# Query and key rows of 14 tokens per partition, and scores, masks and values laid out with heads for batches

## The chip, the core and the metric

The program runs on one core of one Trainium2 chip. The core has five engines that this text speaks of: TensorE (PE; its weight loads are shown as PEld), VectorE (DVE), ScalarE (ACT), GpSimd (POOL) and SyncE (SP), and 16 DMA engines that move data between device memory and the on-chip memory of 128 partitions. Matmuls write to a small second memory, PSUM. The metric is the device time of one execution in microseconds, the median of several runs.

## The reference

Attention with an extra term in the softmax denominator, and then a mixture of experts with soft slots over all its tokens. The shapes: 8 batches, 12 heads, 448 tokens, 64 numbers to a head; 8 experts of 4 slots, hidden size 1024.

```
scores = q @ k^T / 8
m = max(scores, -1);  e = exp(scores - m)
attn = e / (sum(e) + exp(-m) + 1e-9);   a = attn @ v
x = a with heads side by side                     # 3584 x 768
logits = x @ phi                                  # 3584 x 32
d = softmax of logits over tokens;  slot_in = d^T @ x
slot_out[e] = relu(slot_in[e] @ w1[e]) @ w2[e]
out = (softmax of logits over slots) @ slot_out
```

## The kernel before

The work is cut into 24 units. A unit is a pair of batches and a pair of heads, so four attention problems of 448 x 448 at once. Six units make the 12 heads of a pair of batches, after which a "mixture" step (`mixture`) adds those tokens to the running slot sums. The experts run once at the end, and the output is scattered from their results.

The 448 tokens of a batch are held as 64 rows of 7 tokens. A load (`load`, L164 to L169) brings, for one batch and two heads, 64 partitions with two runs of 7 x 64 numbers, one for each head; the second batch goes to partitions 64 to 127. Queries and keys are brought by GpSimd's queue (four loads a unit, two units ahead, converted to 16 bits on the way), values by SyncE's queue (two loads a unit, as 32-bit numbers).

Every unit passes through these stages:

- `stage_T`: TensorE turns the query and key rows (L326: 28 transposes, each of all 128 partitions by 64 columns), VectorE copies the result to `QT` and `KT` (L327). There the partitions are (head, number within the head), and the free axis is (batch, token). The first unit does this batch by batch, as its loads come (L315 to L317).
- `stage_S`, seven steps: each step computes scores of 128 queries against 448 keys for two problems (L340), and VectorE takes the row maximum (L347). In the first six steps the two problems are the two heads of one batch; the seventh, the edge, takes the 64 queries that are left of each batch. A "wide" step (a step that also has values matmuls) uses two matmuls with 128 query columns, any other four with 64.
- `stage_MT`: the maxima are turned, ScalarE copies them (L357), and GpSimd multiplies them with a mask (L364, `base8`), so that a matmul with `select` can add -m to the scores.
- `stage_ST`, seven steps, 11 steps behind `stage_S`: four matmuls add -m (L375), four compute the scores turned (L380), ScalarE takes the exponential (L384).
- `stage_V`: GpSimd copies the values to 16 bits beside a column of ones (L389).
- `stage_AV`: 12 matmuls and 4 edge matmuls per key block multiply the exponentials with the values (L409); the column of ones gives the sum. `stage_AVout`: ScalarE copies the result out (L419).
- `stage_den` and `stage_N`: GpSimd adds the extra term (L425, L426), VectorE takes the reciprocal (L443), GpSimd multiplies (`normalise`, L432 twice and L437).
- `stage_X`: TensorE turns the result (L483), VectorE copies it (L485), for the mixture.

A step is one score step; seven make a unit. The order of all this is written out by hand: `SCH` gives each stage a step counted from its unit's first and a place within the step. The places come in the order small, scores, mid, value, exponentials' step, end, load. Each engine takes its instructions in that order and waits where an input or a buffer isn't ready. `'V': (13, 'mid')` puts the values copy ahead of the two key loads of step 6 of the next unit (`qk`, places value and end); `'den': (19, 'load')` puts the denominators one step ahead of them. Weights come on GpSimd's queue at the places of `WAT`. PSUM is cut into four rotating buffers (`slot`), one of which holds the running product of `stage_AV`.

A matmul of 64 rows by 64 columns uses a quarter of TensorE's array: the rows are given by the partitions of its inputs, the columns by the partitions of its output.

`gate_T` (L593 to L600) writes the gate's probabilities, turned, to `cT`, with two ScalarE copies per mixture.

Of the kernel before, what the change touches and what calls it, by code (L numbers as in the profile page):

```python
# [16 lines left out]
P = 64  # L17
LAG = 11
AV0 = (15, 15, 16, 17, 18, 19, 19)
SCH = {'T': (6, 'value'), 'qk': ((2, 'load'), (1, 'mid'), (6, 'end'), (6, 'value')), 'MT': (6, 'load'), 'V': (13, 'mid'), 'v': ((14, 'load'), (17, 'end')), 'AVout': (19, 'mid'), 'N': ((23, 'value'), (23, 'small')), 'X': (27, 'end'), 'mix': (28, ''), 'den': (19, 'load'), 'lp': (29, 'value'), 'last': (21, 'load'), 'Xlast': (24, 'value'), 'k1': (20, 'mid'), 'k2': (30, 'value'), 'k3': (32, 'small'), 'k4': (34, 'load'), 'Xprev': (25, 'value'), 'T0': (1, 'mid'), 'T1': (4, 'value'), 'Vlast': (12, 'end'), 'MT0': (7, 'mid')}  # L20
# [10 lines left out]
def kernel(  # L31
# [26 lines left out]
    G = E // 4  # L58
    scale = 1.0 / (D ** 0.5)
# [104 lines left out]
    def load(u, t_, src, eng, bs):  # L164
        bp, hp = divmod(u, HP)
# [3 lines left out]
        return t_  # L169

    def load_qk(u, which):

        i, b = divmod(which, 2)
        src, name = ((q, "qr"), (k, "kr"))[i]
        RAW[u, name] = load(u, buf(*(("x", 1) if (u, i) == (1, 1) else ("raw", 2 * u + i))).rearrange("p (h n) -> p h n", h=2), src, nc.gpsimd, (b,))

    def load_v(u, bs=range(2)):
        t_ = buf("vr", 0).bitcast(F32).rearrange("p (h n) -> p h n", h=2)
        RAW[u, "vr"] = load(u, t_, v, nc.sync if u else nc.gpsimd, bs)
# [41 lines left out]
    nmask = const.tile([128, TB], BF16, name="nmask")  # L221
    nc.vector.memset(nmask, 0.0)
    for h in range(2):
        for cols, base, pattern in (
                (nmask[:, ds(0, 2 * C3)].rearrange("p (b c) -> p b c", b=2), C3 * h, [[-TB, 2], [-1, C3]]),
                (nmask[:, ds(2 * C3, 1)], 2 * C3 + TB * h, [[-1, 1]])):
            nc.gpsimd.affine_select(
                out=cols, in_=cols, compare_op=ALU.not_equal, fill=-1.0,
                base=-P * h - base, pattern=pattern, channel_multiplier=1)
# [31 lines left out]
    select = buf("select", 0).rearrange("p (b n) -> p b n", b=2)  # L261

    def shift_masks():
        both = [nmask[:, ds(b * C3, C3)] for b in range(2)]
        edge = nmask[:, ds(2 * C3, 1)]
        nc.gpsimd.tensor_tensor(base8[:, ds(1, 2 * C3)].rearrange("p (c r) -> p c r", r=2),
                                both[0].unsqueeze(2).broadcast_to([128, C3, 2]),
                                both[1].unsqueeze(2).broadcast_to([128, C3, 2]), op=ALU.add)
        for i in (0, TB):
            nc.gpsimd.tensor_copy(base8[:, ds(i, 1)], edge)  # L270
        for b in range(2):
            one = pickb[:, ds(b, 1)]
            nc.gpsimd.tensor_tensor(one, both[b][:, ds(0, 1)], both[b][:, ds(1, 1)], op=ALU.add)
            nc.gpsimd.tensor_tensor(one, one, both[b][:, ds(2, 1)], op=ALU.add)
            nc.gpsimd.tensor_tensor(one, one, edge, op=ALU.add)
        nc.scalar.activation(select, pickb.unsqueeze(2).broadcast_to([128, 2, P]), AF.Copy, scale=-1.0)
# [25 lines left out]
    def stage_T(u, bs_=range(2)):  # L302

        if bs_[0] == 0:
            t_ = buf("qk", u).rearrange("p (i b n) -> p i b n", i=2, b=2)
            QT[u], KT[u], QK[u] = t_[:, 0], t_[:, 1], t_
        t_ = QK[u]
        if u == 0:
            for b in bs_:
                bs = ds(b * P, P)  # L310
                ps = slot([128, 2, 1024], BF16, "T")
                for i, name in enumerate(("qr", "kr")):
                    for t in range(TB):
                        for h in range(2):
                            nc.tensor.transpose(ps[ds(h * D, D), i, part_of(b, t)],  # L315
                                                RAW[u, name][bs, h, ts(t, D)], ident[bs, bs])
                nc.vector.tensor_copy(t_[:, :, b], ps[:, :, ds(0, S)])  # L317
            return
        ps = slot([128, 2, 1024], BF16, "T")
        for i, name in enumerate(("qr", "kr")):  # L320
            r = RAW.pop((u, name))
            for t in range(TB):
                o = (ps[:, i].rearrange("p (b n) -> p b n", b=2)[:, :, ts(t, P)] if t < TB - 1 else
                     ps[:, i, ds(t * P, 2 * P)].rearrange("p (b n) -> p b n", b=2))
                for h in range(2):
                    nc.tensor.transpose(o[ds(h * D, D)], r[:, h, ts(t, D)], ident)  # L326
        (nc.vector.tensor_copy if OPT["T"] == "dve" else nc.scalar.copy)(  # L327
            t_, ps[:, :, ds(0, N2)].rearrange("p i (b n) -> p i b n", b=2))

    def stage_S(u, s):  # L330
        ps = slot([128, 2, 512], kind="S")
        wide = OPT["S"] == "wide" and s < 2 * C3 and u * TB + s in av_steps
        for h in range(2):
            hs = ds(h * D, D)
            for r in range(1 if wide else 2):

                b, o = divmod(s, C3) if s < 2 * C3 else (r, C3)
                o = (o * 128 + r * P + b * P if s < 2 * C3 else o * 128 * (1 - b))
                rs = ds(0, 128) if wide else ds(r * P, P)
                nc.tensor.matmul(ps[rs, h, ds(0, S)], QT[u][hs, b, ds(o, 128 if wide else P)],  # L340
                                 KT[u][hs, b, :], start=True, stop=True)
        m = M[u % 2][:, ds(0, 2 * TB)].rearrange("p (b e) -> p b e", b=2)
        if s < 2 * C3:
            m = m[:, s // C3, ds(0, 2 * C3)].rearrange("p (h c) -> p h c", h=2)[:, :, s % C3]
        else:
            m = m[:, :, 2 * C3]
        nc.vector.tensor_reduce(m, ps[:, :, ds(0, S)], axis=AX.X, op=ALU.max)  # L347
# [22 lines left out]
    def stage_ST(u, t):  # L370
        ps = slot([128, 2, 512], kind="ST")
        for b in range(2):
            for h in range(2):
                hs = ds(h * D, D)
                nc.tensor.matmul(ps[ds(b * P, P), h, ds(0, S)], select[hs, b, :], MD[u][b][hs, :],  # L375
                                 start=True, stop=False)
        for b in range(2):
            for h in range(2):
                hs = ds(h * D, D)
                nc.tensor.matmul(ps[ds(b * P, P), h, ds(0, S)],  # L380
                                 KT[u][hs, b, part_of(b, t)], QT[u][hs, b, :],
                                 start=False, stop=True)
        et = buf("et", u * TB + t).rearrange("p (h n) -> p h n", h=2)
# [3 lines left out]
    def stage_V(u):  # L387
        t_ = buf("v6", u).rearrange("p (h t e) -> p h t e", h=2, e=66)
        nc.gpsimd.tensor_copy(t_[:, :, :, ds(0, D)],  # L389
                              RAW.pop((u, "vr")).rearrange("p h (t d) -> p h t d", t=TB))  # L390
        V65[u] = t_

    def stage_AV(u, ts_, part):
# [3 lines left out]
        for t in ts_:  # L397
# [3 lines left out]
            for h in range(2):  # L401
                for c in (range(C3) if part == 0 else (C3,)):
                    for b in range(2):
                        bs = ds(b * P, P)
                        if c < C3:
                            o, w = av[:, b, ds((h * C3 + c) * 65, 65)], 128
                        else:
                            o, w = av[ds(b * P, P), h, ds(2 * C3 * 65, 65)], P
                        nc.tensor.matmul(o, et[bs, h, ds(c * 128 + b * P if c < C3 else c * 128 * (1 - b), w)],  # L409
                                         V65[u][bs, h, t, ds(0, 65)],  # L410
                                         start=(t == 0 and h == 0 and c == 0),
# [17 lines left out]
    def normalise(eng, x, av, rec):  # L429
        xo = x.rearrange("p s (h d) -> p s h d", h=2)  # L430
        for b in range(2):
            eng.tensor_tensor(  # L432
                xo[:, ds(b * C3, C3)].rearrange("p c h d -> p h c d"),
                av[:, b, ds(0, 2 * C3 * 65)].rearrange("p (h c e) -> p h c e", h=2, e=65)[:, :, :, ds(0, D)],
                rec[:, b, ds(0, 2 * C3)].rearrange("p (h c) -> p h c", h=2)
                   .unsqueeze(3).broadcast_to([128, 2, C3, D]), op=ALU.mult)
        eng.tensor_tensor(xo[:, TB - 1], av[:, :, ds(2 * C3 * 65, D)],  # L437
                          rec[:, :, 2 * C3].unsqueeze(2).broadcast_to([128, 2, D]), op=ALU.mult)
# [60 lines left out]
    def mixture(bp, n, at):  # L499
# [93 lines left out]
        def gate_T():  # L593
            ps = slot([128, 2, 128], BF16)
            for r in range(2):
                nc.tensor.transpose(ps[:, r, :], cr[:, r, :], ident)

            nc.scalar.copy(cT[ds(0, 96), bp, :].rearrange("p (a b q) -> p a b q", a=2, b=2),
                           ps[ds(0, 96)].rearrange("p b (a q) -> p a b q", a=2))
            nc.scalar.copy(cT[ds(96, 32), bp, ds(0, 128)], ps[ds(96, 32), 0, :])  # L600
# [287 lines left out]
```

## Time and profile before

| | us |
|---|---|
| runs | 314.24, 310.84, 313.21 (median 313.21) |
| profiled execution | 315.13 |
| its span, from the first instruction to the last | 313.4 |

The profile comes from one more execution; what its span leaves out, 1.7 us, lies around the program's instructions. In the page, a group of instructions is named by source line, engine and operation, with the memory it writes and reads, the shape, the count, the busy time in all and the mean of one. These groups matter here:

| line, engine | what | count | busy us | mean ns |
|---|---|---|---|---|
| L347 DVE | row maxima of scores | 168 | 179.4 | 1089 |
| L384 ACT | exponentials | 168 | 153.7 | 918 |
| L409 PE | values matmuls | 2688 | 76.6 | 193 |
| L375, L380, L340 PE | matmuls of 448 columns | 672, 672, 452 | 69.9, 66.9, 65.5 | 370, 356, 387 |
| L326 PE | transposes of queries and keys | 644 | 24.2 | 228 |
| L327 DVE | their copy | 23 | 24.9 | 1082 |
| L167 POOL | query and key load issues | 96 | 61.1 | 639 |
| L432, L437 POOL | normalising | 46, 23 | 37.3, 9.1 | 836, 397 |

Busy time of matmuls that overlap is counted once, so the sum over a group is less than count times mean. Idle time of an engine is put down to what released it; "issue" stands for time in which the engine waited for nothing that the profile shows. DMA rows count packets; each packet keeps one of 16 DMA engines busy.

### The profile page before, as it was taken

The page shows a single profiled execution, that of the slowest core. Times are in us where ns is not written, and L with a number is a line of the kernel's source. Part 1 is how long each engine was busy: PE and PEld are TensorE (multiplying, and loading weights), DVE is VectorE, ACT ScalarE, POOL GpSimd, SP SyncE. Part 2 cuts the span into 40 slices and gives each one's busy share as a digit, 9 for nine tenths or more (in the row PEclk, how much of TensorE's full clock was granted, in tenths as well). Part 3 has the DMA queues.
Part 4 walks back from the last instruction along what each step waited for, and adds up shares of the span by engine and source line. Part 5 has one row for each costly group of instructions (what it writes and reads, how often), then busy time and mean ns, then how long its engine had stood idle before and what let it go on. Part 6 is the DMA issues. An engine that isn't in the chain of part 4 may idle for free.

```text
span 313.4 us, 13695 instructions
## 1 busy us (share of the span) xinstructions
PE 271.3 (87%) x6080; PEld 153.6 (49%) x6080; DVE 251.6 (80%) x324; ACT 209.5 (67%) x306; POOL 198.2 (63%) x342
## 2 busy tenths in 40 slices
PE   3689998999889999997999899999999978897660
PEld 2235554555555565654555555555555544453110
DVE  2998998999979899997898899999999525428560
ACT  1127777777767888885776787777968875335351
POOL 8965877798867787799476777798676551200000
PEclk9999999999999999999899999999999999996555
DMA  6999999989989789989598799899999999956997
GB/s 84 178 162 206 172 184 158 199 169 172 172 170 185 150 140 191 207 171 185 102 205 154 132 175 183 154 191 189 171 167 207 192 176 179 202 105 265 424 425 293
DMA packets 29258, 59.12 MB, mean 189 GB/s; under 512 B 4272, under 2 KB 23216, under 8 KB 29200
## 3 DMA queue, kind: packets, MB, share of 16 engines
q0 software_dynamic: 19728, 36.69, 71.2%
q1 hardware_dynamic: 9472, 21.57, 19.8%
q8 instruction: 47, 0.77, 1.0%
q14 instruction: 11, 0.09, 0.1%
HBM read 83.46 MB, written 11.01 MB: 301 GB/s over the span
## 4 chain that ended last, share of the span: by engine, by line
PE 61%; DVE 11%; ACT 9%; issue 6%; POOL 6%; DMA 4%; SPq 0%; ACTq 0%; POOLq 0%; DVEq 0%
PE ps L409 14%; PE ps L340 12%; PE ps L375 11%; PE ps L380 8%; ACT block L384 6%; PE ps L326 5%; DVE m_sb L347 5%; PE ps L645 3%; DMA out_dram<-wres 3%; POOL block L167 2%; PE ps L483 2%; DVE block L327 2%; PE ps L823 2%; ACT wres L830 1%; POOL block L432 1%
## 5 line engine op out<-in xcount | busy, mean ns | idle before, releaser
L347 DVE TENSOR_REDUCE m_sb<-ps 128x2 bf16<-128x896 f32 x168 | 179.4, 1089 | 15.2 <-PE ps L340 9.3
L384 ACT ACTIVATE block<-ps 128x896 bf16<-128x896 f32 x168 | 153.7, 918 | 52.3 <-PE ps L380 45.1
L409 PE MATMUL ps<-block 64*128 64x65 bf16 (+1 forms) x2688 | 76.6, 193 | 4.2 <-issue 4.0
L409 PEld LDWEIGHTS <-block 64*128 64x128 bf16 (+1 forms) x2688 | 67.0, 97 | 22.4 <-issue 5.2
L375 PE MATMUL ps<-block 64*64 64x448 bf16 x672 | 69.9, 370 | 2.8 <-DVE acc L495 0.9
L340 PE MATMUL ps<-block 64*64 64x448 bf16 (+1 forms) x452 | 65.5, 387 | 6.9 <-DVE block L317 1.9
L380 PE MATMUL ps<-block 64*64 64x448 bf16 x672 | 66.9, 356 | 0.0
L340 PEld LDWEIGHTS <-block 64*64 64x64 bf16 (+1 forms) x452 | 22.9, 103 | 52.9 <-issue 41.5
L432 POOL TENSOR_TENSOR block<-block,rec 128x384 bf16<-128x384 f32 x46 | 37.3, 836 | 8.5 <-DVE rec L443 7.1
L375 PEld LDWEIGHTS <-block 64*64 64x64 bf16 x672 | 26.7, 106 | 13.9 <-issue 10.3
L167 POOL DMA_DIRECT2D block<-in_k_dram x48 | 30.4, 636 | 1.9 <-PE ps L326 1.9
L167 POOL DMA_DIRECT2D block<-in_q_dram x48 | 30.7, 641 | 0.8 <-POOLq L872 0.8
L364 POOL TENSOR_TENSOR block<-mt,base 128x512 bf16<-128x512 bf16 x23 | 24.3, 1055 | 5.5 <-ACT mt L357 5.2
L195 POOL DMA_DIRECT2D wres<-in_moe_w_dram x48 | 26.5, 553 | 1.6 <-issue 1.6
L425 POOL TENSOR_TENSOR den<-block,em 128x14 f32<-128x14 f32 x23 | 4.9, 211 | 35.2 <-ACT block L419 35.2
L327 DVE COPY block<-ps 128x1792 bf16<-128x1792 bf16 x23 | 24.9, 1082 | 0.7 <-PE ps L326 0.6
L389 POOL CAST block<-block 128x896 bf16<-128x896 f32 x24 | 22.4, 933 | 4.7 <-DMA block<-in_v_dram 3.4
L326 PEld LDWEIGHTS <-block 128*64 128x64 bf16 x644 | 21.5, 115 | 7.9 <-issue 6.9
L326 PE MATMUL ps<-ident,block 128*64 128x128 bf16 x644 | 24.2, 228 | 0.5 <-issue 0.3
L380 PEld LDWEIGHTS <-block 64*64 64x64 bf16 x672 | 24.2, 107 | 0.2
L419 ACT COPY block<-ps 128x910 f32<-128x910 f32 x22 | 20.2, 918 | 1.6 <-POOL block L437 0.4
L832 DVE TENSOR_SCALAR wres<-ps,acc 128x768 f32<-128x768 f32 (+1 forms) x16 | 14.7, 941 | 7.5 <-PE ps L823 4.7
(130 smaller groups left out, 220.7 us busy)
## 6 DMA issues: line engine op xcount, KB each, us to landing
wres<-in_moe_w_dram POOLq DMA_DIRECT2D x48, 384.0 KB, 5.7
block<-in_v_dram SPq DMA_DIRECT2D x46, 224.0 KB, 5.0
out_dram<-wres SPq DMA_DIRECT2D x11, 768.0 KB, 5.4
block<-in_moe_w_dram POOLq DMA_DIRECT2D x8, 768.0 KB, 9.1
block<-in_q_dram POOLq DMA_DIRECT2D x48, 112.0 KB, 4.2
block<-in_k_dram POOLq DMA_DIRECT2D x48, 112.0 KB, 4.4
out_dram<-wres SPq DMA_DIRECT2D x5, 384.0 KB, 5.1
block<-in_v_dram POOLq DMA_DIRECT2D x2, 224.0 KB, 4.7
```

The source lines that it names most:

```text
L167: eng.dma_start(out=t_[ds(b * P, P), :, :], in_=src[bp * 2 + b, ds(hp * 2, 2)].rearrange("h (p t) d -> p h (t d)", t=TB))
L195: gdma(out=t_[rows, ts(half, HW)], in_=src[rows, ts(half, HW)])
L326: nc.tensor.transpose(o[ds(h * D, D)], r[:, h, ts(t, D)], ident)
L327: (nc.vector.tensor_copy if OPT["T"] == "dve" else nc.scalar.copy)(t_, ps[:, :, ds(0, N2)].rearrange("p i (b n) -> p i b n", b=2))
L340: nc.tensor.matmul(ps[rs, h, ds(0, S)], QT[u][hs, b, ds(o, 128 if wide else P)], KT[u][hs, b, :], start=True, stop=True)
L347: nc.vector.tensor_reduce(m, ps[:, :, ds(0, S)], axis=AX.X, op=ALU.max)
L364: (nc.vector if end_ else nc.gpsimd).tensor_tensor(md.rearrange("p (a r n) -> p a r n", a=4, r=2), mt.rearrange("p (r n) -> p r n", r=2).u ...
L375: nc.tensor.matmul(ps[ds(b * P, P), h, ds(0, S)], select[hs, b, :], MD[u][b][hs, :], start=True, stop=False)
L380: nc.tensor.matmul(ps[ds(b * P, P), h, ds(0, S)], KT[u][hs, b, part_of(b, t)], QT[u][hs, b, :], start=False, stop=True)
L384: nc.scalar.activation(et, ps[:, :, ds(0, S)], AF.Exp, scale=scale)
L409: nc.tensor.matmul(o, et[bs, h, ds(c * 128 + b * P if c < C3 else c * 128 * (1 - b), w)], V65[u][bs, h, t, ds(0, 65)], start=(t == 0 and h ...
L432: eng.tensor_tensor(xo[:, ds(b * C3, C3)].rearrange("p c h d -> p h c d"), av[:, b, ds(0, 2 * C3 * 65)].rearrange("p (h c e) -> p h c e", ...
```

## The change

Queries and keys: a partition now holds 14 tokens of one head. For one batch, 32 partitions belong to the first head and 32 to the second, so a load is a plain matrix of 64 rows of 14 x 64 numbers. The two batches still sit in the two halves of the partitions. Turning therefore has to be done by quarters: 14 blocks for each batch, each from 64 partitions to 64 partitions, 56 transposes of 64 x 64 for queries and keys instead of 28 of 128 x 64. After it the partitions are (batch, number within the head) and the free axis is (head, token). All that follows has heads and batches exchanged: scores steps pair the two batches of one head (in the first unit two heads of one batch, on one half of the partitions), exponentials have partitions (head, key) and free axis (batch, query), values have partitions (head, token row) and free axis (batch, tokens), masks and maxima follow. Values now come by four transfers of 32 partitions a unit. The edge score step takes, for each batch, both heads on one quarter of the array; the edge values matmuls go over all four quarters. In the first unit queries and keys get a PSUM buffer each, and ScalarE copies the keys.

Normalising is two instructions, one for each head. `gate_T` has three copies, since the rows of 32 x 14 tokens have another order. In the order by hand, `V` goes from place mid to place end of step 13, behind the key load of place value, and `den` from step 19 to step 20.

The diff, cut to what is spoken of:

```diff
-SCH = {... 'V': (13, 'mid'), ... 'den': (19, 'load'), ...}
+SCH = {... 'V': (13, 'end'), ... 'den': (20, 'load'), ...}
...
-        for b in bs:
-            eng.dma_start(out=t_[ds(b * P, P), :, :],
-                          in_=src[bp * 2 + b, ds(hp * 2, 2)].rearrange("h (p t) d -> p h (t d)", t=TB))
...
+        nc.gpsimd.dma_start(out=t_[ds(b * P, P), :],
+                            in_=src[bp * 2 + b, ds(hp * 2, 2)].rearrange("h (p t) d -> (h p) (t d)", t=2 * TB))
...
+        for h in hs_:
+            for r in range(2):
+                (nc.sync if u else nc.gpsimd).dma_start(
+                    out=t_[ds(h * P + r * Q, Q), :, :],
+                    in_=v[ds(bp * 2, 2), hp * 2 + h].rearrange("b (p r t) d -> r p b (t d)", r=2, t=TB)[r])
...
-            for t in range(TB):
...
-                for h in range(2):
-                    nc.tensor.transpose(o[ds(h * D, D)], r[:, h, ts(t, D)], ident)
...
+            o = ps[:, i, ds(0, N2)].rearrange("p (h t r q) -> p r t h q", h=2, t=TB, r=2)
+            for t in range(2 * TB):
+                for b in bs_:
+                    bs = ds(b * P, P)
+                    nc.tensor.transpose(o[bs, t // TB, (t + b) % TB], r[bs, ts(t, D)], ident[bs, bs])
+            if u == 0:
+                bs = ds(bs_[0] * P, P)
+                (nc.scalar.copy if i else nc.vector.tensor_copy)(
+                    t_[bs, i], ps[bs, i, ds(0, N2)].rearrange("p (h n) -> p h n", h=2))
...
+        a, c = divmod(s, C3)
+        for r in range(1 if wide else 2):
+            for x in range(2):
+                b, h = (r, x) if s == 2 * C3 else (x, a) if u else (a, x)
+                bs, rs = ds(b * P, P), ds(0, 128) if wide else ds(r * P, P)
+                o = c * 128 + r * P + b * P if s < 2 * C3 else C3 * 128 * (1 - b)
+                nc.tensor.matmul(ps[rs, x, ds(0, S)], QT[u][bs, h, ds(o, 128 if wide else P)],
+                                 KT[u][bs, h, :], start=True, stop=True)
...
-            for h in range(2):
+            for b in range(2):
                 for c in (range(C3) if part == 0 else (C3,)):
-                    for b in range(2):
-                        bs = ds(b * P, P)
+                    for h in range(2):
+                        hs = ds(h * P, P)
...
-        for b in range(2):
+        for h in range(2):
             eng.tensor_tensor(
...
+                xo[:, :, h, :],
+                av[:, h, ds(0, TB * 65)].rearrange("p (m e) -> p m e", e=65)[:, :, ds(0, D)],
+                rec[:, h, :].unsqueeze(2).broadcast_to([128, TB, D]), op=ALU.mult)
...
-            nc.scalar.copy(cT[ds(0, 96), bp, :].rearrange("p (a b q) -> p a b q", a=2, b=2),
-                           ps[ds(0, 96)].rearrange("p b (a q) -> p a b q", a=2))
...
+            for a in range(2):
+                nc.scalar.copy(cT[ds(0, 96), bp, ts(a, 128)].rearrange("p (b q r) -> p b q r", b=2, r=2),
+                               ps[ds(0, 96), :, ts(a, P)].rearrange("p b (r q) -> p b q r", r=2))
```

More of the change, by code (lines that the diff above doesn't have):

```diff
@@ L260 @@
     pickb = const.tile([128, 2], BF16, name="pickb")
-    select = buf("select", 0).rearrange("p (b n) -> p b n", b=2)
+    select = buf("select", 0).rearrange("p (h n) -> p h n", h=2)
     def shift_masks():
-        both = [nmask[:, ds(b * C3, C3)] for b in range(2)]
-        edge = nmask[:, ds(2 * C3, 1)]
+        both = [nmask[:, ds(h * C3, C3)] for h in range(2)]
+        edge = [nmask[:, ds(2 * C3 + h, 1)] for h in range(2)]
         nc.gpsimd.tensor_tensor(base8[:, ds(1, 2 * C3)].rearrange("p (c r) -> p c r", r=2),
@@ L269, in shift_masks @@
         for i in (0, TB):
-            nc.gpsimd.tensor_copy(base8[:, ds(i, 1)], edge)
-        for b in range(2):
[L272 to L275, printed above, removed]
+            nc.gpsimd.tensor_tensor(base8[:, ds(i, 1)], edge[0], edge[1], op=ALU.add)
+        for h in range(2):
+            one = pickb[:, ds(h, 1)]
+            nc.gpsimd.tensor_tensor(one, both[h][:, ds(0, 1)], both[h][:, ds(1, 1)], op=ALU.add)
+            nc.gpsimd.tensor_tensor(one, one, both[h][:, ds(2, 1)], op=ALU.add)
+            nc.gpsimd.tensor_tensor(one, one, edge[h], op=ALU.add)
         nc.scalar.activation(select, pickb.unsqueeze(2).broadcast_to([128, 2, P]), AF.Copy, scale=-1.0)
@@ L304, in stage_T @@
         if bs_[0] == 0:
-            t_ = buf("qk", u).rearrange("p (i b n) -> p i b n", i=2, b=2)
+            t_ = buf("qk", u).rearrange("p (i h n) -> p i h n", i=2, h=2)
             QT[u], KT[u], QK[u] = t_[:, 0], t_[:, 1], t_
         t_ = QK[u]
-        if u == 0:
-            for b in bs_:
-                bs = ds(b * P, P)
+        ps = None if u == 0 else slot([128, 2, 1024], BF16, "T")
+        for i, name in enumerate(("qr", "kr")):
+            r = RAW[u, name]
+            if u == 0:
                 ps = slot([128, 2, 1024], BF16, "T")
-                for i, name in enumerate(("qr", "kr")):
-                    for t in range(TB):
-                        for h in range(2):
[L315 to L328, printed above, removed]
+            o = ps[:, i, ds(0, N2)].rearrange("p (h t r q) -> p r t h q", h=2, t=TB, r=2)
[3 more added lines that the diff above has]
+                    nc.tensor.transpose(o[bs, t // TB, (t + b) % TB], r[bs, ts(t, D)], ident[bs, bs])
+            if u == 0:
+                bs = ds(bs_[0] * P, P)
+                (nc.scalar.copy if i else nc.vector.tensor_copy)(
+                    t_[bs, i], ps[bs, i, ds(0, N2)].rearrange("p (h n) -> p h n", h=2))
+        if u:
+            (nc.vector.tensor_copy if OPT["T"] == "dve" else nc.scalar.copy)(
+                t_, ps[:, :, ds(0, N2)].rearrange("p i (h n) -> p i h n", h=2))
     def stage_S(u, s):
@@ L332, in stage_S @@
         wide = OPT["S"] == "wide" and s < 2 * C3 and u * TB + s in av_steps
[L333 to L344, printed above, removed]
+        a, c = divmod(s, C3)
[6 more added lines that the diff above has]
+                                 KT[u][bs, h, :], start=True, stop=True)
+        m = M[u % 2][:, ds(0, 2 * TB)].rearrange("p (h e) -> p h e", h=2)
+        if u and s < 2 * C3:
+            m = m[:, a, ds(0, 2 * C3)].rearrange("p (b c) -> p b c", b=2)[:, :, c]
         else:
-            m = m[:, :, 2 * C3]
+            m = m[:, :, s]
         nc.vector.tensor_reduce(m, ps[:, :, ds(0, S)], axis=AX.X, op=ALU.max)
@@ L400, in stage_AV @@
             av, et = AV[u], ET[u, t]
-            for h in range(2):
+            for b in range(2):
                 for c in (range(C3) if part == 0 else (C3,)):
-                    for b in range(2):
-                        bs = ds(b * P, P)
+                    for h in range(2):
+                        hs = ds(h * P, P)
                         if c < C3:
-                            o, w = av[:, b, ds((h * C3 + c) * 65, 65)], 128
+                            o, w = av[:, h, ds((b * C3 + c) * 65, 65)], 128
                         else:
                             o, w = av[ds(b * P, P), h, ds(2 * C3 * 65, 65)], P
-                        nc.tensor.matmul(o, et[bs, h, ds(c * 128 + b * P if c < C3 else c * 128 * (1 - b), w)],
-                                         V65[u][bs, h, t, ds(0, 65)],
-                                         start=(t == 0 and h == 0 and c == 0),
+                        nc.tensor.matmul(o, et[hs, b, ds(c * 128 + b * P if c < C3 else c * 128 * (1 - b), w)],
+                                         V65[u][hs, b, t, ds(0, 65)],
+                                         start=(t == 0 and b == 0 and c == 0),
                                          stop=(t == TB - 1), skip_group_check=True)
```

58 lines of the change are left out of this document (27 added, 31 removed).

## The prediction

> **What bounds the kernel now.** I read the page's busy shares first, then VectorE's timeline through one undisturbed unit (a unit is two batches by two heads; 24 run in a row), TensorE's timeline in the same place, the chain of waits, and last the records of single instructions and DMA packets.
>
> ```profile
> PE 271.3 (87%) x6080; PEld 153.6 (49%) x6080; DVE 251.6 (80%) x324; ACT 209.5 (67%) x306; POOL 198.2 (63%) x342
> DMA  6999999989989789989598799899999999956997
> q0 software_dynamic: 19728, 36.69, 71.2%
> q8 instruction: 47, 0.77, 1.0%
> ```
>
> No engine is full over the span, but the DMA engines nearly are, and the instruction queue q8 shares them.
>
> ```profile
> 136.59 5.53 DVE L347 TENSOR_REDUCE m_sb<-ps 128x2 bf16<-128x896 f32 x5
> 142.03 1.08 DVE L327 COPY block<-ps 128x1792 bf16<-128x1792 bf16 x1
> 143.03 0.61 DVE L485 COPY block<-ps 128x896 bf16<-128x896 bf16 x1
> 143.67 2.09 DVE L347 TENSOR_REDUCE m_sb<-ps 128x2 bf16<-128x896 f32 x2
> ```
>
> VectorE works through a unit without a gap: from the first reduction of unit 13 (134.44) to that of unit 14 (143.67) are 9.23 us, and the best units all take 9.22 to 9.24. Back to back a reduction takes 1.00 us; here the starts within the unit are 1.01, 1.15, 1.04, 1.05, 1.15 and 1.19 apart, so TensorE sets the pace in the middle.
>
> ```profile
> 139.61 0.72 PE L409 MATMUL ps<-block 64*128 64x65 bf16 x28
> 140.17 0.22 PE L409 MATMUL ps<-block 64*64 64x65 bf16 x4
> 140.35 0.42 PE L380 MATMUL ps<-block 64*64 64x448 bf16 x4
> 140.54 0.42 PE L340 MATMUL ps<-block 64*64 64x448 bf16 x4
> 140.98 0.97 PE L326 MATMUL ps<-ident,block 128*64 128x128 bf16 x28
> ```
>
> Four 64x64 matmuls of 448 columns on four different quarters of the array finish in 0.42 us together, with about 0.19 between successive ones on one quarter. The 28 transposes (0.97) start when the fifth reduction frees their buffer and end 0.08 before the sixth one, so they are just hidden.
>
> ```profile
> 85.42 1.21 issue
> ...
> 139.79 0.54 PE ps L409 x28
> 140.98 0.97 PE ps L326 x28
> ...
> 145.00 1.66 issue
> ```
>
> This, from the chain of waits, is what breaks the rhythm. Over units 1 to 22 the periods sum to 222.2 us, 19 more than 22 of 9.23. Some is the mixture's work, but "issue" names no producer. Numbering TensorE's instructions by start, eight pauses over 0.45 us between 25 and 258 us end exactly at a number that is 193 above a multiple of 256 (the 1729th, 3265th, 6081st and so on); less 0.1 each for ordinary spacing they add to 7.7 us. q8 moved 47 packets of 16 KB, one per 256 instructions of TensorE. After each such boundary the next packet starts 0.5 to 4.5 us later (mean 2.2), while the 16 engines are about fully busy with loads, takes 1.0, and the new page runs about 1.4 us after it landed. A page of 256 lasts 5.25 us in a good unit (450 instructions in 9.23), so a packet landing more than 3.85 after the boundary stops TensorE. The last pause shown also preceded 3.4 us of half clock; unit 14 took 12.41.
>
> **The change, part by part.** Its sum is made against the profiled execution: 315.13 us, of which 313.4 are the span, 1.9 above the median of the runs shown.
>
> *First unit.* Its transposes now use one quarter per batch, so they can't pair. The cold row in place is
>
> ```profile
> 4.73 0.96 PE L315 MATMUL ps<-ident,block 64*64 64x64 bf16 x28 [4.73 <-DVE ident L215]
> 6.41 0.96 PE L340 MATMUL ps<-block 64*64 64x448 bf16 x8 [0.72 <-DVE block L317]
> ```
>
> Up to 24 us four score matmuls take 0.59 instead of 0.38, so this is a slower clock. 28 in 0.96, less 0.24 for the last to finish, is 26.7 ns each for pairs, so 53 alone: 28 take 1.5 + 0.2 instead of 0.96. VectorE copies queries, ScalarE keys (0.905, L485's row on ScalarE), which ends 0.9 after the last transpose instead of 0.62. The first scores then run in two rounds of 0.37. First reduction: +0.75 +0.3 +0.37, less 0.3 for four shorter load issues ahead of the identity, +1.1. The second batch repeats part of it, so VectorE's unbroken stretch (from 14.25) begins 1.1 to 2.0 later; TensorE may warm up earlier and give back up to 0.5. I take +1.6, bounds +0.6 and +2.2.
>
> *Transposes, 23 units.* 56 of 64x64 replace 28 of 128x64: 28 more pairs of weight load and matmul per unit. Two diagonal quarters work side by side: the four values matmuls of L409 on such quarters start in pairs, 3 ns within a pair, 30 between pairs, and 28 wider ones at L409 take 0.54, 13 ns apiece. So 28 pairs at 29 ns + 0.2 = 1.03 against 0.97; 0.06 lies under the 0.08 of cover. Zero. Without the cover it is 1.4 us over 23 units.
>
> *Edge scores (seventh step).* The four matmuls now use two quarters instead of four: +0.19 before the sixth reduction can begin, in front of VectorE. The edge values matmuls use four instead of two, saving 0.03 each, 0.06 in the step ahead. Net +0.13 there; the other five save up to 0.15 a unit, but only where TensorE and not VectorE's 1.00 sets the pace. I take +0.05 a unit, +1.0; bounds -2 (all savings tell) and +3 (none do).
>
> *GpSimd and SyncE.* Loads keep their number but have half the rows (641 ns; the 64-row weight load L195 takes 553), so up to 8 us of issue go, and normalising is two instructions of 448 instead of 384+384+128 (by the rows 1.89 us against 2.07). The denominators move past a key load, the values cast and another key load; their 35.2 us of waiting for ScalarE's L419 end. GpSimd has slack: zero. Behind the first key load, which waits for the transposes, now stands the cast: done near 143.6 instead of 143.05, values matmuls at 144.24. If that 0.6 went, TensorE would wait at the first values step. The reciprocal (145.68) needs denominators done near 144.65; the key-maximum product, now after them, is read steps later. Values come by four transfers on SyncE instead of two, two issues of 0.6 later; they landed 3 us before the cast. Zero.
>
> *Mixtures, last unit.* gate_T gets a third ScalarE copy (its rows: 361+258 become about 3 x 260), +0.16, where a reduction waited for it three times: +0.5. In the last unit the first transposes must now wait for both normalising instructions: +0.3.
>
> *TensorE's pages.* 506 instructions in 9.23 us make a page last 4.67. Against it the DMA engines are relieved: query and key packets took 1,301 of their 5,014 us, 12,288 of 896 B written at 88 ns (median). A packet of 1792 B, by the line through 88 and the 146 ns of 3584 B packets, takes 107, and there are half as many: 32 us less per engine. A queue built from the trace's issue times and packet times (it follows the observed delays only with correlation 0.55) then waits 0.4 less. Summing landing + 1.4 - page time over the 43 packets of 25 to 258 us, where positive, gives 10.6 before (7.7 seen, 0.73 of it). With 4.67 and 0.4 less it is 13.0, with 12% more pages 14.6, of which 0.73 is 10.6: +3. Bounds: no relief +9, a full microsecond of it -3. The Trainium skill, "Runtime: NRT & Kernel Launch", section "Instruction fetch mechanics", also has blocks of 256 instructions, but says that crossing one is mostly hidden, because instructions are dispatched more slowly than blocks come. The 7.7 us here speak against it; by it this term is zero and the sum +3.4.
>
> Sum: 1.6 + 0 + 1.0 + 0 + 0.8 + 3 = **+6.4**: 321.5 for the profiled execution, **319.6** on the runs' median.
>
> **Rivals.**
> - *The relief wins.* Lighter loads land the pages sooner than TensorE uses them. It decides when packets land under about 3.3 us after the boundary (4.67 - 1.4) nearly always; today 21 of 43 do. For it: the engines are at nine tenths throughout, so a tenth less load can cut waiting by more than a tenth. Against: weight loads, which stand before most late packets, stay. Pages -3, the half-clock window of unit 14 (1.3) gone, edges -2, units' start +1.6, copies +0.8: -4, 309.
> - *Terms cancel.* Pages cost nothing more, edges gain a little: +1.6 + 0.8 - 1 to + 1, 314.5. A pause is partly covered already where VectorE is behind.
> - *Pages become the bound.* Packets of twice the size take twice as long, so the change saves no DMA time (then it doesn't do what it says): pages +9, edges +3, the rest 2.4: 327.5. For it: the 6144 B packets take 474 ns, in proportion to 896 B at 70; against it: 3584 B at 146.
> - *Small transposes don't overlap.* At L315's cold 26.7 ns each, 56 take 1.7, 0.75 more than 0.97, less 0.08, times 23: +15 on the sum, 335. For it, these are the trace's only long run of 64x64 transposes, if a cold one. Against it stand the 13 ns of L409. The Trainium skill, "TensorE: Matmul & The Clock Gate", section "Wait — 56ns, not 53.3ns?", has a floor of about 25 ns from start to start, which would give nearly this; the trace undercuts it on separate quarters.
>
> **How the numbers follow.** Forecast 0.40, relief 0.20, cancelling 0.20, pages as bound 0.13, no overlap 0.07. One per cent (3.1 us; the three runs differ by 3.4) is about what can be told from no change: faster 0.20, same 0.20, slower 0.60. The range reaches from the relief case, 309, to the page-bound case, 328; outside are the transposes (0.07) and the ends of those two. The forecast's own range is 314 to 325.
>
> **What would show it.** Right: the gap before the sixth reduction grows from 1.19 to about 1.3; transposes last 1.0; the first reduction comes near 8.1 instead of 7.05; q8 has 52 packets, with ten or more pauses at multiples of 256; query and key packets take 100 to 110 ns. Wrong: transposes of 1.5 us, packets of 176 ns, pauses that vanish, or a first values matmul that waits for the cast.

## The result, and the profile after

The changed kernel took 322.23 us (median of 4 runs, 320.60 to 323.12), the kernel before 312.45 beside it (4 runs): a ratio of 1.030, with a 95% interval from 1.025 to 1.034, so 7.9 to 10.7 us slower. The profiled execution took 322.24 with a span of 320.5; that of before took 315.13 with 313.4.

The rows of the page that answer to those shown of before:

```profile
PE 272.5 (85%) x6724; PEld 157.7 (49%) x6724; DVE 251.5 (78%) x323; ACT 211.6 (66%) x312; POOL 187.0 (58%) x321
DMA  6999896998998698989997999899979979965997
q0 software_dynamic: 13648, 36.69, 66.0%
q8 instruction: 52, 0.85, 1.0%
```

VectorE is busy for as long as before, TensorE's matmuls 1.2 us longer, its weight loads 4.1 and ScalarE 2.1; GpSimd is busy 11 us less. The span is 7 us longer, so most of it went into waiting. GpSimd's queue has 6,080 packets fewer, yet its share fell only from 71.2 to 66.0%. q8, which brings the program text of TensorE in instruction pages of 256 instructions, moved 52 of them instead of 47.

VectorE in an undisturbed unit (unit 14), from its timeline:

```profile
152.24 2.09 DVE L345 TENSOR_REDUCE m_sb<-ps 128x2 bf16<-128x896 f32 x2
154.25 0.23 DVE L438 RECIPROCAL rec<-den 128x14 f32<-128x14 f32 x1
154.45 4.39 DVE L345 TENSOR_REDUCE m_sb<-ps 128x2 bf16<-128x896 f32 x4
159.06 1.10 DVE L345 TENSOR_REDUCE m_sb<-ps 128x2 bf16<-128x896 f32 x1 [0.22 <-PE ps L338]
160.07 1.08 DVE L326 COPY block<-ps 128x1792 bf16<-128x1792 bf16 x1
```

and TensorE in the same place:

```profile
157.53 0.72 PE L407 MATMUL ps<-block 64*128 64x65 bf16 x32
158.09 0.36 PE L373 MATMUL ps<-block 64*64 64x448 bf16 x4
158.28 0.36 PE L378 MATMUL ps<-block 64*64 64x448 bf16 x4
158.47 0.55 PE L338 MATMUL ps<-block 64*64 64x448 bf16 x4
158.89 0.98 PE L320 MATMUL ps<-ident,block 64*64 64x64 bf16 x51
```

The edge scores (L338) last 0.55 instead of 0.42, and VectorE waits 0.22 for them: the gap from the sixth reduction of a unit to the seventh went from 1.19 or 1.20 to 1.31. The transposes (51 in this row, 5 more just behind it) take 1.07 in all, against 0.97. A unit in which nothing else happens takes 9.32 us instead of 9.23. That is a small part of the loss. The larger one stands in the chain of waits:

```profile
32.95 0.77 PE ps L320 x45
33.72 1.55 issue
...
43.94 0.92 PE ps L320 x55
44.85 1.16 issue
...
65.33 0.86 PE ps L320 x51
66.64 1.07 issue
```

TensorE stops in the middle of, or right behind, the transposes, at the 961st, 1473rd and 2497th of its instructions: all 193 above a multiple of 256, the page boundaries. Numbered in this way, the traces split as follows; a second pair of profiles, e11 and e12 below, stands beside the first. A pause is one over 0.45 us at a boundary between 25 and 267 us, less 0.1 of ordinary spacing. TensorE's instructions are its matmuls, their weight loads and a few waits for semaphores.

| us | before | after | before again | after again |
|---|---|---|---|---|
| first reduction of unit 1 | 16.24 | 17.36 | 16.25 | 17.36 |
| first reduction of unit 1 to that of unit 23 | 222.2 | 226.7 | 221.8 | 226.9 |
| last values matmul ends | 260.7 | 268.1 | 259.0 | 268.6 |
| pauses at page boundaries, sum (count) | 7.7 (8) | 13.0 (15) | 6.7 (8) | 15.8 (16) |
| last values matmul to first expert matmul | 8.8 | 9.1 | 8.8 | 9.1 |
| span | 313.4 | 320.5 | 312.1 | 321.0 |

Up to the last values matmul the changed kernel is 7.5 and 9.6 us behind; the pauses differ by 5.4 and 9.1. In each of the 15 pauses of the changed kernel TensorE goes on 1.2 to 1.5 us after a q8 packet has landed, and in the 8 of the kernel before 1.3 to 1.7 us after: a pause ends when its page has come.

### The profile page after: what moved, and what is told of

Same layout as the page of the kernel before. It is cut to its first block, busy times and chain, and to the rows that moved or that the text cites. A ratio compares the mean times of both kernels' runs of the same rounds, so it can differ in the third digit from the quotient of the medians.

```text
span 320.5 us, 14988 instructions
## 1 busy us (share of the span) xinstructions
PE 272.5 (85%) x6724; PEld 157.7 (49%) x6724; DVE 251.5 (78%) x323; ACT 211.6 (66%) x312; POOL 187.0 (58%) x321
## 4 chain that ended last, share of the span: by engine, by line
PE 48%; DVE 18%; issue 11%; POOL 7%; ACT 7%; DMA 6%; SPq 1%; ACTq 0%; POOLq 0%; DVEq 0%
PE ps L407 12%; PE ps L338 11%; DVE m_sb L345 9%; PE ps L373 8%; PE ps L378 7%; ACT block L382 5%; PE ps L320 4%; DMA out_dram<-wres 4%; DVE block L326 4%; PE ps L642 3%; POOL block L170 2%; DMA block<-in_v_dram 2%; POOL block L387 2%; POOL block L430 2%; DVE block L480 1%
## 5 line engine op out<-in xcount | busy, mean ns | idle before, releaser
L338 PE MATMUL ps<-block 64*64 64x448 bf16 (+1 forms) x452 | 71.7, 386 | 7.2 <-DVE block L326 3.2
L407 PE MATMUL ps<-block 64*128 64x65 bf16 (+1 forms) x2688 | 72.1, 195 | 2.1 <-issue 1.2
L407 PEld LDWEIGHTS <-block 64*128 64x128 bf16 (+1 forms) x2688 | 62.6, 97 | 20.9 <-issue 4.9
L373 PE MATMUL ps<-block 64*64 64x448 bf16 x672 | 65.6, 363 | 4.5 <-issue 1.3
L378 PE MATMUL ps<-block 64*64 64x448 bf16 x672 | 65.6, 355 | 2.9 <-issue 2.8
L338 PEld LDWEIGHTS <-block 64*64 64x64 bf16 (+1 forms) x452 | 26.8, 104 | 53.9 <-issue 42.2
L170 POOL DMA_DIRECT2D block<-in_k_dram x48 | 24.9, 520 | 45.7 <-PE ps L320 45.7
L430 POOL TENSOR_TENSOR block<-block,rec 128x448 bf16<-128x448 f32 x46 | 42.2, 940 | 9.7 <-DVE rec L438 6.4
L320 PE MATMUL ps<-ident,block 64*64 64x64 bf16 x1344 | 31.0, 198 | 8.3 <-DVE ident L218 4.4
L320 PEld LDWEIGHTS <-block 64*64 64x64 bf16 x1344 | 29.7, 113 | 12.1 <-DMA block<-in_q_dram 4.3
L373 PEld LDWEIGHTS <-block 64*64 64x64 bf16 x672 | 24.6, 106 | 15.3 <-issue 12.4
L378 PEld LDWEIGHTS <-block 64*64 64x64 bf16 x672 | 22.1, 108 | 4.6 <-issue 4.3
L820 PE MATMUL ps<-wres,cT 32*128 32x384 bf16 x56 | 15.0, 458 | 5.7 <-DVE wres L829 3.4
```

The costliest lines, as they stand in the source:

```text
L170: nc.gpsimd.dma_start(out=t_[ds(b * P, P), :], in_=src[bp * 2 + b, ds(hp * 2, 2)].rearrange("h (p t) d -> (h p) (t d)", t=2 * TB))
L320: nc.tensor.transpose(o[bs, t // TB, (t + b) % TB], r[bs, ts(t, D)], ident[bs, bs])
L338: nc.tensor.matmul(ps[rs, x, ds(0, S)], QT[u][bs, h, ds(o, 128 if wide else P)], KT[u][bs, h, :], start=True, stop=True)
L373: nc.tensor.matmul(ps[ds(h * P, P), b, ds(0, S)], select[bs, h, :], MD[u][b][bs, :], start=True, stop=False)
L378: nc.tensor.matmul(ps[ds(h * P, P), b, ds(0, S)], KT[u][bs, h, part_of(b, t)], QT[u][bs, h, :], start=False, stop=True)
L407: nc.tensor.matmul(o, et[hs, b, ds(c * 128 + b * P if c < C3 else c * 128 * (1 - b), w)], V65[u][hs, b, t, ds(0, 65)], start=(t == 0 and b ...
```

## The experiments

The theory going in: the change costs time because it gives TensorE 56 more instructions a unit, so that pages run out before the next one has come through the queue of loads. Its rivals are the parts of the change that do work in another way: the edge step, the first unit, the order on GpSimd. e1 to e4 take these apart. A ratio is to the kernel before as it ran beside that batch of runs (median 311.3 us for e1 to e4, 313.4 for e8, 314.8 for e9 and e10); the changed kernel was not run again beside them, and its own ratio, 1.030, is from the first comparison.

**e1: instructions alone.** The kernel before, with 56 transposes of 64x64 on four quarters:

```diff
-                for h in range(2):
-                    nc.tensor.transpose(o[ds(h * D, D)], r[:, h, ts(t, D)], ident)
+                for h in range(2):
+                    for b in range(2):
+                        bs = ds(b * P, P)
+                        nc.tensor.transpose(ps[ds(h * D, D), b, ds(i * S + (t + b) % TB * P, P)],
+                                            r[bs, h, ts(t, D)], ident[bs, bs])
...
-            t_, ps[:, :, ds(0, N2)].rearrange("p i (b n) -> p i b n", b=2))
+            t_, ps[:, :, ds(0, N2)].rearrange("p b (i n) -> p i b n", i=2))
```

> The kernel before, with only its transposes changed: 56 of 64x64 on all four quarters of TensorE instead of 28 of 128x64, so that it issues as many TensorE instructions a unit (506) as the changed kernel while loads, layout, edge step and first unit stay. Page theory (more instructions empty a page of 256 sooner, and TensorE waits for the next one): pauses at page boundaries between 25 us and the end of the attention rise from 8 (7.7 us) to 12 or more (11 to 13 us), 52 packets in q8, time +3 to +6 us over the kernel before. Rival (the layout, the edge step and the first unit cost the 9.3 us, the pages nothing): time within 1 us of the kernel before, or a little faster because four quarters turn sooner (0.6 us instead of 0.97).

Measured: 1.035 of the kernel before (1.029 to 1.042), 322.7 against 311.3 us, as slow as the whole change. Pauses: 13 with 15.7 us. Two stretches of TensorE's timeline, a disturbed one first:

```profile
84.90 0.63 PE L326 MATMUL ps<-ident,block 64*64 64x64 bf16 x54
86.63 0.22 PE L326 MATMUL ps<-ident,block 64*64 64x64 bf16 x2 [1.09 <-issue]
...
140.01 0.64 PE L326 MATMUL ps<-ident,block 64*64 64x64 bf16 x56
```

The transposes by themselves got a third faster (0.64 us for 56). But in the first of the two TensorE stops two transposes short of the end for 1.09 us, and VectorE's copy behind it is late by as much. The expectation had +3 to +6 us; it is +11. Loads, layout, edge step and first unit are untouched, so none of those is needed for a loss of this size. The sum of the pauses is not the whole price here: behind three of them (1.9, 1.4 and 1.9 us) the granted clock was 0.5 for 13.6 us in all, from 34.1, 98.9 and 256.0 us. Between 25 and 260 us the kernel before has one such stretch (3.4 us, the one named in the prediction), and so has the changed kernel (3.4 us from 48.0).

**e2: the edge step back on four quarters.**

```diff
-                b, h = (r, x) if s == 2 * C3 else (x, a) if u else (a, x)
+                b, h = (x, r) if s == 2 * C3 else (x, a) if u else (a, x)
```

> The changed kernel with its edge scores on four quarters of the array again, as before: each matmul takes another batch and head than it should, so the row maxima of the edge queries are those of other rows. Edge theory (two matmuls one behind the other on a quarter hold the sixth reduction back): the gap before the seventh reduction of a unit falls from 1.31 to about 1.15, a unit is 0.13 to 0.2 shorter, time 3 to 4 us under the changed kernel (ratio to the kernel before 1.018 to 1.02). Rival (pages and the first unit are the cost): the gap falls, but the time stays within 1 us of the changed kernel (1.027 to 1.033).

Measured: the gap falls to 1.13, but the time is 1.039 of the kernel before (1.031 to 1.046), not below the changed kernel (medians 323.6 and 322.2 us). The pauses are 13.6 us, as in the changed kernel (13.0 and 15.8). The edge theory is out as the main cost; the time is even above what the rival gave, and where the edge step's small gain went isn't shown.

**e3: the old order on GpSimd.**

```diff
-'V': (13, 'end') ... 'den': (20, 'load')
+'V': (13, 'mid') ... 'den': (19, 'load')
```

> The changed kernel with the values copy and the denominators at their old places (values copy ahead of both key loads, denominators one step earlier). Theory that the new places are free: within 1 us of the changed kernel (ratio 1.027 to 1.033), GpSimd's wait for the transposes (45.7 us in the changed kernel) shrinks and its wait for ScalarE's copy of the product comes back (35 us). Rival (GpSimd, held by a key load that waits for the transposes, delays loads and copies behind it): 2 to 4 us faster than the changed kernel (1.017 to 1.023).

Measured: 1.034 (1.028 to 1.040); GpSimd's wait for the transposes is gone and it waits 41.1 us for ScalarE's copy instead. The median, 321.9 us, is within 1 us of the changed kernel's: the order costs and brings nothing that shows here.

**e4: the first unit like all others.**

```diff
-            if u == 0:
-                ps = slot([128, 2, 1024], BF16, "T")
...
-                b, h = (r, x) if s == 2 * C3 else (x, a) if u else (a, x)
+                b, h = (r, x) if s == 2 * C3 else (x, a)
...
-    stage_T(0, (0,))
-    at(*SCH["T0"], lambda: stage_T(0, (1,)))
+    stage_T(0)
```

> The changed kernel with its first unit treated as all others: it waits for the loads of both batches, then turns all at once and pairs batches in the scores. First-unit theory (its work on one half of the array costs 1.1 us up to the second unit): four loads of 0.55 must be issued and land, so the first reduction comes near 8.5 instead of 8.03, but the following ones are 1.00 apart, and the second unit's first reduction comes at 16 to 17 instead of 17.36: 0 to 1.5 us faster than the changed kernel (1.025 to 1.03). Rival: the second batch's loads come so late that it is as slow or slower (1.03 to 1.035).

Measured: 1.043 (1.035 to 1.051). The first reduction comes at 9.98 instead of 8.03, and though five follow 1.00 apart, it isn't made up: the first reduction of unit 1 comes at 18.26 instead of 17.36. The rival held in its direction, and the way by halves is the better one here; but only 0.9 us of the loss stands at the first unit, and why the time is above the rival's 1.035 isn't shown.

**e5 to e7: the loads in front of the pages taken away.** Three kernels issue 46 of 48 weight loads only after the attention. Each was run once; the whole times, 391.8, 393.4 and 392.1 us, are long because the end waits for the weights:

```diff
-        at(*place, lambda i=i, part=part: load_w(i, part))
+        at(*(place if i == 0 and part < 2 else (182, "load")), lambda i=i, part=part: load_w(i, part))
```

> The kernel before with 46 of its 48 expert weight loads issued only after the attention, so that query, key and value loads and the pages have the DMA engines to themselves; the end then waits for the weights and the whole time (some 90 us more) says nothing. Read from the first reduction of unit 1 to that of unit 23 (222.2 us in the kernel before). Page theory: pages land within 3 us of their boundary, no pause over 0.45 us at a boundary, 214 to 217 us. Rival (the pauses come from the instruction stream, not from waiting behind loads): pauses stay, 220 us or more.

> The same in the changed kernel (226.7 us from unit 1 to unit 23). Page theory: at most one pause, and only the edge step's 0.1 us a unit over the run of the kernel before with late weights: 216 to 219.5 us. Rival (layout and order cost by themselves): 4 us or more above it.

> The same in the kernel before with 56 quarter transposes (227.6 us from unit 1 to unit 23). Page theory: within 1 us of the kernel before with late weights, since only the waiting for pages told the two apart. Rival (64x64 transposes cost by themselves): still 3 us or more above it.

| from unit 1 to unit 23, us | weights as they are | weights late | pauses then |
|---|---|---|---|
| kernel before | 222.2 | 215.0 (e5) | 1 (0.7 us) |
| changed kernel | 226.7 | 216.1 (e6) | none |
| before with quarter transposes | 227.6 | 214.9 (e7) | none |

This settles that the pauses are waits for pages behind loads. The windows view gives the DMA engines' share (the number before the last one in a row) and shows what was taken away; the changed kernel, as it is and with late weights:

```profile
17.30:244.00 226.70, 208.22 (x5648) 125.29 (x5649) 204.44 (x233) 168.97 (x245) 157.72 (x258) 0.99 0.89 168
```

```profile
17.30:233.40 216.10, 205.06 (x5648) 124.82 (x5649) 203.71 (x233) 168.70 (x245) 134.79 (x214) 1.00 0.53 99
```

The same matmuls (5,648) and the same VectorE work run in 10.6 us less once the DMA engines are 53% busy instead of 89%. The wait from a boundary to the next packet falls from 2.3 to 1.2 us or less (a few packets that start just ahead of their boundary are missed by this count). The late loads also take 44 instructions and 23 us of work from GpSimd, but that is not the reason: between 25 and 260 us of the changed kernel TensorE and its weight loads wait for GpSimd for 1.8 us in all. Who waited is seen in VectorE's copy of the transposes, in the groups by line of e1 and of e7, which differ in the weight loads alone:

```profile
L328 DVE COPY block<-ps 128x1792 bf16<-128x1792 bf16 x22 | 23.8, 1082 | 4.5 <-PE ps L326 4.5
```

```profile
L328 DVE COPY block<-ps 128x1792 bf16<-128x1792 bf16 x22 | 23.8, 1081 | 0.0
```

4.5 us of waiting for TensorE are down to nothing. And what is left between e6 and e5, 1.0 us over 22 units (1.7 without e5's one pause), is the price of the edge step and the wider layout in a stream without pauses.

**e8: smaller weight loads.** The kernel before, each weight load cut in two:

```diff
-    pieces = 4
+    pieces = 8
...
-        half, part = divmod(part, 2)
-        rows = ds(part * P, P)
+        half, part = divmod(part, 4)
+        rows = ds(part * 32, 32)
...
+    places = [(n + 2 * k, where) for n, where in WAT for k in range(2)]
```

> The kernel before with each weight load cut into two of 32 rows, the second two steps later, so that less stands before a page at a time. Page theory: pages wait about 0.3 us less in the mean, the 7.7 us of pauses fall to 3 to 6, time 1 to 4 us under the kernel before (ratio 0.987 to 0.997). Rival (48 more issues of 0.5 us on GpSimd and more queueing eat it up): same or up to 2 us slower (1.0 to 1.007).

Measured: 1.003 (0.999 to 1.006). The pauses sum to 6.4 us, but pages wait as long as before (2.4 us in the mean). The rival held. Perhaps as much stands before a page as ever, only in smaller pieces; no run here shows it.

**e9 and e10: weight loads placed by the page boundaries**, in the kernel before and in the changed one:

```diff
-WAT = ((1, 'end'), (4, 'load'), (8, 'end'), (11, 'load'), (15, 'end'), (18, 'load'), ...
+WAT = ((1, 'end'), (4, 'load'), (6, 'load'), (8, 'end'), (11, 'load'), (14, 'load'), (19, 'mid'), ...
```

> The kernel before with 41 of its weight loads moved to the place in the order by hand that follows a page boundary (the boundaries stand at fixed instructions of TensorE), so that a page is asked for before the next weight load and not behind it. Page theory: the wait of a page falls from 2.26 us to under 1.8, the pauses from 7.7 us to under 4, time 2 to 5 us under the kernel before (ratio 0.984 to 0.994). Rival (what waits is not the weight load in front; query, key and value loads hold the page as long): wait and time unchanged (0.997 to 1.003).

> The same in the changed kernel, by its own boundaries (44 of 48 weight loads). Page theory: 4 to 8 us under the changed kernel (ratio to the kernel before 1.005 to 1.017), since its pages cost it 10.6 us. Rival: unchanged (1.027 to 1.035).

Measured: e9 1.016 (1.006 to 1.025), e10 1.035 (1.027 to 1.042): neither is faster. Both are poor tests. A place in the order by hand isn't a time: GpSimd runs ahead of the scores, and in e9 16 of the 48 loads were issued 3 us or less before the next boundary, not right behind one. In e9 the pauses fell to 3.5 us and units 1 to 23 took 219.2 us, 3 less, but the last unit's values came late, as its chain of waits shows:

```profile
244.77 12.09 DMA block<-in_v_dram
257.00 0.94 POOL block L389
257.99 1.09 PE ps L409 x28
```

That load took 12.1 us. It was issued between weight loads that had been pushed to the end (at 244.0, 244.6 and 247.3 us; in the kernel before the last one left at 242.8), and TensorE's granted clock was then 0.5 for 10.2 us from 253.1. From the first reduction of unit 23 to the last values matmul e9 took 29.3 us instead of 22.3, more than the 3 it had gained. In e10 the pauses stayed (15.4 us). Whether weight loads timed well, at both ends, would beat the kernel before was not settled; no kernel here does.

**e11 and e12: both kernels profiled again.**

> The kernel before, unchanged, profiled once more, because its first profiled execution took 315.1 us against a median of 312.5. Theory that pauses at page boundaries differ from one execution to the next and make that difference: an execution nearer the median has 4 to 6 us of pauses instead of 7.7, at the same places in the count (193 above a multiple of 256) but not at the same ones, and 218 to 221 us from unit 1 to unit 23 instead of 222.2. Rival (the pauses are fixed by the program): the same boundaries, 7 to 8.5 us.

> The changed kernel, unchanged, profiled once more. Its first profiled execution was at its median: 10 to 13 us of pauses, 226 to 228 us from unit 1 to unit 23. With the run before it, the difference between the two kernels in pauses should come near 6 us, not the 3.9 of the first pair; rival: 3 to 4.5 again.

Measured: 6.7 us of pauses in e11, at other boundaries than the first time (two in common, the 3265th and the 3521st), and 15.8 in e12, above the expected 10 to 13. From unit 1 to unit 23 are 221.8 and 226.9 us. (The 3.9 of the expectation counts the first pair up to 258 us; the table counts up to 267 us, which makes it 5.4.) So the program fixes where a pause can be, and the run decides which of them happen. The kernel before's pauses fell less than expected (6.7, not 4 to 6); the difference between the kernels is 9.1 in this pair, above the 6 that was expected.

## Why the prediction was right, and one term too small

The direction and the main mechanism were right: slower, with pages as the largest term. The median, 322.2, lies in the range, 2.6 above the 319.6 forecast: 9.3 us by the ratio against 6.4. Two of the prediction's sums are slightly off: 28 pairs at 29 ns and 0.2 us make 1.01 and not 1.03, and the terms of the cancelling rival give 314.6 to 316.6, not 314.5. Neither bears on the outcome. By its steps:

- *First unit*: taken +1.6, measured +1.1 at the first reduction of unit 1 (16.24 to 17.36), in the bounds. The first reduction itself came at 8.03 (forecast 8.1).
- *Transposes*: 1.07 us for 56 (forecast 1.03), on two quarters side by side, 16 ns apiece at the full clock. No cost in an undisturbed unit. The rival with 1.7 us is out.
- *Edge scores*: gap 1.31 (forecast 1.3; the prediction numbers the reductions from 0, so its sixth is the seventh here); +1.0 us over 22 units between e5 and e6, as taken, with the rest of the layout in it. That nothing is gained by taking it away again in the real kernel (e2) was not foreseen and isn't explained.
- *GpSimd and SyncE*: taken at zero. GpSimd waits 45.7 us for the transposes and no value matmul pays for it (0.3 us of waiting for the cast in all); e3 agrees.
- *Mixtures and last unit*: +0.3 for the last unit was right (8.8 to 9.1 us from the last values matmul to the experts). The +0.5 for `gate_T` was not: its copies take 263+263+258 ns as priced, but no reduction waits for them any more.
- *TensorE's pages*: taken +3, bounds -3 and +9. The pauses rose by 5.4 us in one pair of profiles and by 9.1 in the other, 7.2 in the mean. This term was mis-sized, and its failed step is the relief of the DMA engines. "A packet of 1792 B, by the line through 88 and the 146 ns of 3584 B packets, takes 107": it took 154 (median; mean 182). The line joins two kinds of packets. Query and key packets are read as 32-bit numbers and written as 16-bit ones; the 32 packets of 3584 B are values of the first unit, which stay 32-bit numbers. A new query packet also reads 3584 B, so the row of 146 ns was nearly its price, and not a point far beyond it. So half as many packets of twice the size saved about 170 us of engine time instead of 510. SyncE's value packets, as many as before, took 73 us more (624 against 551), so all 16 engines together were busy 101 us less, 6 us for each and not 32. The forecast wait of 0.4 us less became 0.0 in the first pair (2.3 and 2.3) and 0.3 in the second (2.4 and 2.1). Without relief the same sum gave +9; the mean of what was measured lies between. That the missing relief alone makes the difference isn't shown: the second pair had most of the forecast relief in its waits and yet the larger rise in pauses. So the rival "pages become the bound" was nearer in its premise (packets of twice the size take 1.75 times as long, and 13% of their engine time is saved), the row that it held against itself spoke for it, and it was wrong in adding 3 us for edges.

Page boundaries and pauses are read from the count of instructions, the 52 packets and the place of the gaps; that the load on the DMA engines is the reason is shown by e5 to e7. Fewer packets land very late (over 3.85 us after the boundary) in the changed kernel, 10 of 47 against 16 of 44; why is not explained. More of them matter because a page of 256 is used up sooner: by the prediction's 4.67 - 1.4 the limit is now about 3.3 us, and 23 of 47 land later than that.

## What to carry to other kernels

Count the instructions that a change adds to the engine that issues most of them, and not only their busy time: here 1,288 more TensorE instructions cost 3% though they ran side by side with others, and even where they shortened the work itself (e1). Number the engine's instructions in the trace: gaps at a fixed distance in that count, with nobody named as releaser, were here waits for the program text, and they went away when the DMA engines were 53 to 55% busy instead of 89 to 94%. To see what such waits cost, move the bulk loads out of the way and compare what is left.

## What the hardware showed that was not expected

- Instruction pages of TensorE queue behind the kernel's own loads: 2.0 to 2.4 us of waiting in the mean with the DMA engines 89 to 94% busy (both kernels and e1), at most 1.4 with 53 to 55% (e5 to e7), and a pause of up to 2.3 us (e3) when a page of 256 is used up first.
- DMA packets that convert from 32 to 16 bits took 88 ns for 896 B written, 154 for 1792 B and 474 for 6144 B (medians): nearly in proportion to size, so that longer rows save little engine time here. One that reads 3584 B and writes 1792 took about as long as one of 3584 B that isn't converted (146 ns).
- 64x64 transposes ran at 16 ns apiece on two quarters of the array and at 8 ns (56 in 0.64 us, of which 0.2 is the last one's own time) on four.
